# Moving four last-DFT calls of batch 0 out of the transform stage and into the first token tiles

## The chip, the cores and the metric

One core of one Trainium2 chip (runs are compared with runs of the same rounds). The metric is the device time of one execution in microseconds (us). PE is TensorE (matmuls), PEld its weight loads, ACT is ScalarE, DVE is VectorE, POOL is GpSimd, SP is SyncE. "L512" is a line of the kernel. All executions counted here were fast, with a granted TensorE clock of 0.995 to 1.0.

## The reference, cut to what matters

```python
def _attn_ref(x, w_r, w_i, b_r, b_i):            # x: 8 x 3008 x 256
    X = np.fft.rfft(x, axis=1)
    Yr = Xr @ w_r - Xi @ w_i + b_r               # and Yi likewise
    Yr = np.sign(Yr) * np.maximum(np.abs(Yr) - lam, 0.0)
    return np.fft.irfft(Yr + 1j * Yi, n=3008, axis=1)

def _moe_ref(x, w_in, w_out, s, b):              # x: 24064 tokens x 256
    r = np.maximum(x @ w_in, 0.0)                # 256 x 2048
    return (s * (r * r) + b) @ w_out             # 2048 x 256
```

The transforms of length 3008 are done as 94 x 32 by matmuls with DFT tables. "The last DFT" is the final step of the inverse transform; its output `yt` is what the token part reads.

## The kernel before

Batch 0 is transformed first, with only the first units of batch 1 beside it ("the transform stage", up to the first token matmul at 45.56 us). After that come 48 token tiles of 16 slots each. In every slot two matmuls (L781) run, and about four output matmuls (L852) of the tile before. Every second slot ends with one Relu on ACT (L788) and one square (L795 on DVE or L792 on ACT) for both slots. Units of the next batches' transforms are spread over the slots.

The calls that the change moves, cut:

```python
        def last_dft(ec, n):                     # 4 matmuls of 96 columns, 1 evacuation of 128x384
            if ec and n >= HW:                   # HW = 16
                ps = one_bank()                  # pool psf, 2 banks
            elif ec or n >= HW:
                ps = any_bank()                  # psm, psf or psa in turn
            else:
                ps = other_bank() if n % 8 else one_bank()
            for j in range(4):
                ...                              # L512
            evac(yt[:, ec, n : n + 4, :], ..., 384)
...
            for n in {1: (0, 4), 2: (8, 12), 4: (16, 20, 24, 28)}.get(k, ()):
                last_dft(0, n)
...
        rest = [lambda n=n: turn(1, n) for n in range(HW, N2, 4)]
        rest += [lambda n=n: last_dft(1, n) for n in range(HW, N2, 4)]
...
    load.update(act=0.0, dve=0.0)                # at the start of the token tiles
...
    schedule(17, 10, rest[4:])                   # spread over slots 17 to 26
```

Who empties a bank is decided while the program is written, by a running tally of estimated load:

```python
    load = {"act": 0.0, "dve": 0.0}

    def evac(dst, src, cols, scale=None):
        ta, td = 0.17 + cols / 1200.0, 0.15 + cols / 960.0
        if load["act"] + ta <= load["dve"] + td:
            load["act"] += ta
            ...                                  # copy on ScalarE
        load["dve"] += td
        ...                                      # copy on VectorE
...
        # the square of a token tile, same tally
        if load["act"] + 0.25 + w / 600.0 < load["dve"]:
            ...                                  # L792, ScalarE
        else:
            ...                                  # L795, VectorE
```

Of the kernel before, what the change touches and what calls it, by code (L numbers as in the profile page):

```python
# [16 lines left out]
N2 = 32  # L17
# [79 lines left out]
def kernel(  # L97
# [17 lines left out]
    DC = D // P  # L115
# [3 lines left out]
    HW = N2 // 2  # L119
# [45 lines left out]
# [4 lines that stand above are left out]
            if scale is None:  # L169
                return None, nc.scalar.copy(out=dst, in_=src)  # L170
            return None, nc.scalar.mul(out=dst, in_=src, mul=scale)
        load["dve"] += td
        if scale is None:
            return nc.vector.tensor_copy(out=dst, in_=src), None
        return nc.vector.tensor_scalar_mul(out=dst, in0=src, scalar1=scale), None
# [8 lines left out]
    def any_bank():  # L184

        turn_of[0] += 1
        if "h" in pools:
            return (other_bank, one_bank)[turn_of[0] % 2]()
        return (mix_bank, one_bank, mix_bank, other_bank)[turn_of[0] % 4]()
# [4 lines left out]
    def one_bank():  # L194
        return fpool.tile([P, 512], F32, name="psf", tag="psf")

    def other_bank():
        return apool.tile([P, 512], F32, name="psa", tag="psa")
# [128 lines left out]
    def place_f(q):  # L327

        for a in range(2):
            r = slice(64 * a, 64 * a + 64)  # L330
            copy = nc.scalar.copy if a else nc.vector.tensor_copy
            copy(out=blocks(F_t)[r, q, :, a], in_=F_c[r, q])
            nc.vector.tensor_scalar_mul(
                out=blocks(F_2[0])[r, q, 0, a], in0=F_c[r, q, 1], scalar1=-1.0
            )
            nc.vector.tensor_copy(out=blocks(F_2[0])[r, q, 1, a], in_=F_c[r, q, 0])
# [26 lines left out]
    def first_batch():  # L363
# [52 lines left out]
        def mix(ec, u):  # L416

            g = vpool.tile([P, 4, 2, P], F16, name="g0", tag="v")
            gs[(ec, u)] = g
            for half in range(2):  # L420
                ps = mix_bank().rearrange("p (j r e) -> p j r e", j=2, r=2)
                for j in range(2):
                    q = 4 * u + 2 * half + j
                    for dc in range(DC):
                        nc.tensor.matmul(  # L425
                            ps[:, j], ut[:, dc, 4 * q : 4 * q + 4, :],
                            W_t[:, dc, :, ec * P : (ec + 1) * P],
                            start=(dc == 0), stop=(dc == DC - 1),
                        )
                if half:  # L430
                    on_act = nc.scalar.copy(out=g[:, 2:4], in_=ps)
                    load["act"] += 0.58
                else:
                    on_dve = nc.vector.tensor_tensor(
                        out=g[:, 0:2], in0=ps,
                        in1=b_g[:, :, ec * P : (ec + 1) * P].unsqueeze(1).to_broadcast(
                            [P, 2, 2, P]
                        ),
                        op=ALU.add,
                    )  # L440
                    load["dve"] += 0.69
            return on_dve, on_act

        def fwd_dft(ec, u):
            ps = one_bank().rearrange("p (j e) -> p j e", j=4)
            g = gs.pop((ec, u))
            for j in range(4):
                q = 4 * u + j
                if j == 2:
                    nc.tensor.matmul(  # L450
                        ps[:, 2:4], sel_t,
                        b_h[:, ec * P : (ec + 1) * P].unsqueeze(1).to_broadcast([P, 2, P]),
                        start=True, stop=False, skip_group_check=True,
                    )
                for r, f in enumerate((F_t[:, q, :], F_2[q // H][:, q % H, :])):
                    nc.tensor.matmul(  # L456
                        ps[:, j, :], f, g[:, j, r, :], start=(r == 0 and j < 2),
                        stop=(r == 1), skip_group_check=True,
                    )
            pos = mpool.tile([P, 4, P], F32, name="m", tag="m")  # L460
            nc.scalar.activation(out=pos, in_=ps, func=AF.Relu, bias=neg_lam)
            z = gpool.tile([P, 4, P], F16, name="z", tag="gt")
            nc.vector.scalar_tensor_tensor(  # L463
                out=z, in0=ps, scalar=LAM, in1=pos, op0=ALU.add, op1=ALU.min
            )
            load["act"] += 0.69
            load["dve"] += 0.69
            zt[(ec, u)] = z

        def inv_dft(ec, u):  # L470
            ps = other_bank()
            z = zt.pop((ec, u))
            for j in range(4):
                nc.tensor.matmul(
                    ps[:, j * P : (j + 1) * P], z[:, j, :], T_t[:, 4 * u + j, :],
                    start=True, stop=True,
                )
            evac(
                vt[:, ec, :, 16 * u : 16 * u + 16],
                ps.rearrange("p (k n) -> p n k", n=N2), 512,  # L480
            )
# [4 lines left out]
        def turn(ec, n):  # L486

            ps = mix_bank() if ec == 0 else any_bank() if n < HW else one_bank()
            for j in range(4):
                nc.tensor.matmul(  # L490
                    ps[0:96, j * P : j * P + P], vt[:, ec, n + j, :], eye_t,
                    start=True, stop=True,
                )
            h, k = divmod(n, HW)
            evac(
                vs[(0, h)][:, k : k + 4, ec * P : (ec + 1) * P],
                ps[0:96].rearrange("p (j e) -> p j e", e=P), 512,
            )
# [2 lines left out]

        def last_dft(ec, n):

            if ec and n >= HW:
                ps = one_bank()
            elif ec or n >= HW:
                ps = any_bank()
            else:
                ps = other_bank() if n % 8 else one_bank()
            for j in range(4):  # L510
                h, k = divmod(n + j, HW)
                nc.tensor.matmul(  # L512
                    ps[:, j * 96 : j * 96 + 96],
                    vs[(0, h)][:, k, ec * P : (ec + 1) * P], C_t,
                    start=True, stop=True,
                )
            evac(
                yt[:, ec, n : n + 4, :],
                ps[:, 0:384].rearrange("p (j n) -> p j n", n=96), 384,
            )  # L520
# [3 lines left out]
        def some(n):  # L524
            for _ in range(n):
                if more:
                    more.pop(0)()

        steps = [(ec, u) for ec in range(DC) for u in range(U)]
        for i in range(2 * U + 2):  # L530
            if i < 2 * U:
                left = mix(*steps[i])
            if i == 0:
                with tc.issue_after(left[0].ins), tc.issue_after(left[1].ins):
                    place_f(slice(4, H))
            if 0 <= i - 1 < 2 * U:
                fwd_dft(*steps[i - 1])
            if 0 <= i - 2 < 2 * U:
                inv_dft(*steps[i - 2])
            k = i - U - 2  # L540
            if 0 <= k < 4:
                turn(0, 8 * k)
                turn(0, 8 * k + 4)
            for n in {1: (0, 4), 2: (8, 12), 4: (16, 20, 24, 28)}.get(k, ()):
                last_dft(0, n)
            if i >= 2 * U:
                some(3)
            if i == 9:

                gate = nc.gpsimd.tensor_copy(out=low[0:1, 0, 0:1], in_=vt[0:1, 1, 0, 0:1])  # L550
                with tc.issue_after(gate.ins):
                    make_w_g()
                    make_bounds()
                    sum_w_out()
# [4 lines left out]
        turn(1, 12)  # L559
        some(1)  # L560
        last_dft(1, 0)
        last_dft(1, 4)
        some(2)
        last_dft(1, 8)
        last_dft(1, 12)

        rest = [lambda n=n: turn(1, n) for n in range(HW, N2, 4)]
        rest += [lambda n=n: last_dft(1, n) for n in range(HW, N2, 4)]
        return rest, more


# [303 lines left out]
    def schedule(start, span, units):  # L875
        for i, u in enumerate(units):
            plan.setdefault(start + (i * span) // len(units), []).append(u)

    with tc.tile_pool(name="psm", bufs=4, space=bass.MemoryType.PSUM) as pool:
        pools["m"] = pool  # L880
        rest, more = first_batch()
# [10 lines left out]
            mark[tl[1]] = i * MC  # L892
    schedule(0, 10, more)
    schedule(10, 6, rest[:4])
    schedule(17, 10, rest[4:])
    plan.setdefault(14, []).append(make_bias)
    plan.setdefault(18, []).append(load_x_2)
    schedule(24, 42, s23_units(1))
# [53 lines left out]
```

## Time and profile before

| | |
|---|---|
| time, median | 846.8 us (846.37 to 847.73, 6 runs) |
| PE, DVE, ACT busy shares | 99%, 82%, 76% |
| first token matmul (L781) | 45.56 us |
| evacuations of the four moved calls | two on DVE, two on ACT, 38.25 to 40.07 us |
| squares on DVE, on ACT | 319, 65 |

The groups of the page that show how the token work is split (line, engine, operation, output<-input, count; then busy us, mean ns of one; then idle time before them and what ended it):

```profile
L788 ACT ACTIVATE rt<-psh 128x1024 f32<-128x1024 f32 (+2 forms) x384 | 387.2, 1009 | 120.2 <-PE psh L781 118.8
L795 DVE TENSOR_TENSOR gt<-rt 128x1024 f16<-128x1024 f32 (+2 forms) x319 | 382.3, 1202 | 94.4 <-ACT rt L788 93.4
L792 ACT ACTIVATE gt<-rt 128x1024 f16<-128x1024 f32 (+2 forms) x65 | 68.2, 1050 | 0.9
```

Both engines spend much of the token stage waiting for PE: PE is the bound there. The rest of the profile is read in the prediction.

### The profile page before, as it was taken

The numbers are of one execution on the slowest core, as the hardware profiler recorded it, in microseconds if no ns is written. First come the engines' busy times: TensorE is split into PE (matmuls) and PEld (weight loads), VectorE is DVE, ScalarE is ACT, GpSimd is POOL, SyncE is SP. The second block draws the span as 40 slices with busy tenths as digits, with TensorE's granted clock in tenths as the row PEclk, the third lists the DMA queues.
The fourth block names the chain that finished last, engine by engine and source line by source line (L and its number), as shares of the span: only waits on it lengthen the run. The fifth ranks groups of instructions, "written<-read, shape, count | busy, mean of one in ns | idle before, by whom it ended". The sixth has DMA issues, their size and how long they took to land.

```text
span 844.6 us, 17119 instructions
## 1 busy us (share of the span) xinstructions
PE 835.1 (99%) x6654; PEld 601.3 (71%) x6654; DVE 694.7 (82%) x1034; ACT 640.6 (76%) x862; POOL 45.9 (5%) x73
## 2 busy tenths in 40 slices
PE   8999999999999999999999999999999999999998
PEld 7857767777677766777677776777667777766765
DVE  5999987888888988888888888798978888776674
ACT  5987887778778877788777787778877778666673
POOL 4630000000000001000000000000000000000000
PEclk9999999999999999999999999999999999999999
DMA  7955467224851367324761247613354223411111
GB/s 200 181 151 118 119 161 199 74 77 98 202 156 54 103 171 188 93 70 107 189 174 50 81 101 196 172 43 90 106 152 125 59 78 97 113 33 38 38 44 50
DMA packets 105939, 96.06 MB, mean 114 GB/s; under 512 B 9607, under 2 KB 97675, under 8 KB 104515
## 3 DMA queue, kind: packets, MB, share of 16 engines
q1 hardware_dynamic: 99362, 80.55, 32.9%
q0 software_dynamic: 6496, 14.42, 10.6%
q8 instruction: 52, 0.85, 0.4%
q14 instruction: 29, 0.23, 0.1%
HBM read 53.52 MB, written 46.66 MB: 119 GB/s over the span
## 4 chain that ended last, share of the span: by engine, by line
PE 92%; ACT 3%; DVE 2%; DMA 1%; issue 1%; POOL 0%; DVEq 0%; ACTq 0%; POOLq 0%
PE psa L852 38%; PE psh L781 37%; PE psf L647 4%; PE psf L582 3%; PE psf L633 2%; PE psf L677 2%; PE psf L618 2%; PE psf L730 2%; ACT rt L788 1%; DMA x<-in_x_dram 1%; PE psm L425 1%; POOL x L213 0%; ACT yt L170 0%; DVE z L463 0%; PE psf L456 0%
## 5 line engine op out<-in xcount | busy, mean ns | idle before, releaser
L788 ACT ACTIVATE rt<-psh 128x1024 f32<-128x1024 f32 (+2 forms) x384 | 387.2, 1009 | 120.2 <-PE psh L781 118.8
L795 DVE TENSOR_TENSOR gt<-rt 128x1024 f16<-128x1024 f32 (+2 forms) x319 | 382.3, 1202 | 94.4 <-ACT rt L788 93.4
L852 PE MATMUL psa<-w_out_t,gt 128*128 128x256 f16 (+1 forms) x3024 | 454.4, 272 | 0.1
L852 PEld LDWEIGHTS <-gt 128*128 128x128 f16 (+1 forms) x3024 | 300.9, 101 | 186.6 <-issue 1.1
L781 PE MATMUL psh<-yt,w_in 128*128 128x512 f16 (+1 forms) x1344 | 396.8, 378 | 0.2 <-ACT rt L788 0.2
L781 PEld LDWEIGHTS <-w_in 128*128 128x128 f16 x1536 | 142.7, 98 | 26.2 <-issue 1.2
L862 DVE SCALAR_TENSOR_TENSOR ost<-psa,s_bc,bias_bc 128x512 f32<-128x512 f32 (+2 forms) x97 | 71.1, 733 | 9.6 <-PE psa L852 7.9
L792 ACT ACTIVATE gt<-rt 128x1024 f16<-128x1024 f32 (+2 forms) x65 | 68.2, 1050 | 0.9
L652 DVE TENSOR_TENSOR ring<-psf,s 128x512 f16<-128x512 f32 x84 | 57.6, 685 | 3.3 <-PE psf L647 3.2
L170 ACT CAST v<-psf 128x512 f16<-128x512 f32 x77 | 44.8, 582 | 19.4 <-PE psf L677 19.4
L170 ACT CAST xf<-psf 128x512 f16<-128x512 f32 x79 | 46.3, 586 | 8.8 <-PE psf L618 8.8
L781 PE MATMUL psh<-tail,w_in 128*128 128x512 f16 (+1 forms) x192 | 52.1, 353 | 0.0
L170 ACT CAST u<-psf 96x512 f16<-96x512 f32 x74 | 42.8, 580 | 11.2 <-PE psf L582 10.9
L647 PE MATMUL psf<-W_g,xf 128*128 128x256 f16 x336 | 50.4, 273 | 0.0
L170 ACT CAST yt<-psf 128x480 f16<-128x480 f32 (+2 forms) x76 | 39.0, 520 | 14.7 <-PE psf L730 14.2
L213 POOL DMA_DIRECT2D x<-in_x_dram x36 | 18.8, 527 | 432.9 <-PE psf L582 431.7
L582 PE MATMUL psf<-x,A_t 94*96 94x512 f16 x102 | 38.9, 382 | 1.0 <-ACT yt L170 0.6
L658 DVE TENSOR_TENSOR ring<-ring,high 128x512 f16<-128x512 f16 x84 | 35.6, 423 | 2.3
L659 DVE TENSOR_TENSOR ring<-ring 128x512 f16<-128x512 f16 x84 | 35.6, 423 | 2.1
L657 DVE TENSOR_TENSOR ring<-ring,low 128x512 f16<-128x512 f16 x84 | 35.5, 422 | 1.6
L647 PEld LDWEIGHTS <-xf 128*128 128x128 f16 x336 | 32.9, 98 | 4.1 <-issue 0.2
L730 PE MATMUL psf<-C_t,vs 96*128 96x96 f16 x448 | 33.2, 205 | 0.0
(100 smaller groups left out, 508.6 us busy)
## 6 DMA issues: line engine op xcount, KB each, us to landing
out_dram<-ost SPq DMA_DIRECT2D x152, 128.0 KB
ud<-u SPq DMA_DIRECT2D x28, 384.0 KB
us<-ud SPq DMA_DIRECT2D x28, 384.0 KB
vd<-v SPq DMA_DIRECT2D x42, 256.0 KB
vs<-vd SPq DMA_DIRECT2D x14, 768.0 KB
x<-in_x_dram POOLq DMA_DIRECT2D x28, 376.0 KB, 6.3
ring<-ring SPq DMA_DIRECT2D x280, 32.0 KB
out_dram<-ost SPq DMA_DIRECT2D x16, 120.0 KB
```

Of the source, the lines that this page charges most:

```text
L170: return None, nc.scalar.copy(out=dst, in_=src)
L582: nc.tensor.matmul(ps[0:96, :], A_t[0:N1, :], x16[(b, c)][0:N1, j * D : (j + 2) * D], start=True, stop=True,)
L647: nc.tensor.matmul(ps[:, r, :], xt[:, 2 - r, dc], W_g[:, dc, r], start=(dc == 0), stop=(dc == DC - 1),)
L652: nc.vector.tensor_tensor(out=t, in0=ps, in1=hold[i // 2][:, i % 2].unsqueeze(1).to_broadcast([P, 2, D]), op=ALU.add,)
L658: nc.vector.tensor_tensor(out=m, in0=m, in1=high, op=ALU.min)
L730: nc.tensor.matmul(ps[:, j * 96 : (j + 1) * 96], vs[(b, h)][:, k, ec * P : (ec + 1) * P], C_t, start=True, stop=True,)
L781: nc.tensor.matmul(o, w_in_t[dc][:, mc * P : (mc + 1) * P], r, start=(dc == 0), stop=(dc == DC - 1),)
L788: nc.scalar.activation(out=rt[:, :, 0:w], in_=ps[:, :, 0:w], func=AF.Relu)
L792: nc.scalar.activation(out=gt[:, :, 0:w], in_=rt[:, :, 0:w], func=AF.Square)
L795: nc.vector.tensor_tensor(out=gt[:, :, 0:w], in0=rt[:, :, 0:w], in1=rt[:, :, 0:w], op=ALU.mult)
L852: nc.tensor.matmul(ps[0:size, h, :], gts[(ti, mc // 2)][:, mc % 2, sub * size : (sub + 1) * size], w_out_t[:, mc, :], start=(mc == 0), sto ...
L862: nc.vector.scalar_tensor_tensor(out=ost[0:size, 0:k], in0=ps[0:size, 0:k], scalar=s_bc[0:size], in1=bias_bc[0:size].unsqueeze(1).to_broad ...
```

## The change

The intent: the transform stage is limited by evacuations, and four of its last-DFT calls are not needed until the fourth token tile (slot 48). So they join the four calls that already lie in the slots. They use the two psf banks there, and the list is spread over 16 slots instead of 10.

```diff
-            if ec and n >= HW:
+            if n >= HW:
                 ps = one_bank()
-            elif ec or n >= HW:
+            elif ec:
                 ps = any_bank()
...
-            for n in {1: (0, 4), 2: (8, 12), 4: (16, 20, 24, 28)}.get(k, ()):
+            for n in {1: (0, 4), 2: (8, 12)}.get(k, ()):
                 last_dft(0, n)
...
-        rest += [lambda n=n: last_dft(1, n) for n in range(HW, N2, 4)]
+        rest += [lambda n=n, e=e: last_dft(e, n) for n in range(HW, N2, 4) for e in range(DC)]
...
-    schedule(17, 10, rest[4:])
+    schedule(17, 16, rest[4:])
```

## The prediction

> **What bounds the kernel now.** I read the page's first part, then busy time by stretch, then the chain that ended last, then the engines' timelines from 30 to 76 us. Columns of the windows view: stretch, length, then busy time and instruction count of PE, PEld, DVE, ACT and POOL, granted clock, DMA share, GB/s.
>
> ```profile
> PE 835.1 (99%) x6654; PEld 601.3 (71%) x6654; DVE 694.7 (82%) x1034; ACT 640.6 (76%) x862; POOL 45.9 (5%) x73
> 30.00:40.00 10.00, 9.79 (x138) 8.63 (x137) 9.78 (x18) 9.83 (x21) 7.68 (x9) 1.00 1.22 195
> 60.00:70.00 10.00, 9.89 (x87) 7.11 (x86) 8.76 (x14) 6.93 (x11) 2.96 (x8) 1.00 0.81 150
> ```
>
> The two stretches have different limits although PE reads 98 to 99% in both. From 30 to 40 us (batch 0's transforms, where the four moved calls end) DVE and ACT are both full, 9.78 and 9.83 of 10 us. From 60 to 70 us (slots about 21 to 34 of the token tiles) ACT has 3.1 us free and DVE 1.2. To see whether PE is really full I replaced its busy time by what its instructions occupy back to back: in an unbroken run, four matmuls of 96 columns take 0.17 us from start to start, one of 256 takes 0.109, one of 512 takes 0.216. Against the starts in the timeline this leaves about 2.2 us of PE holes from 31.5 to 46 us, 1.6 us from 46 to 76, and only 3.3 us in all of 76 to 845. So the time is the PE work plus some holes early on, and a change to the order of early work can act only through those holes.
>
> The chain of waits (start, length, what) shows the first stretch led by evacuations and the later one by PE:
>
> ```profile
> 38.54 0.60 DVE z L463
> 39.14 0.93 DVE yt L174 x2
> 40.07 0.60 DVE u L174
> 40.67 0.61 DVE vt L174
> ...
> 44.85 0.38 PE psf L582
> 45.23 0.22 PE psa L582
> 45.45 0.27 PE psf L582
> 45.72 0.88 PE psh L781 x4
> ...
> 61.91 0.86 ACT rt L788
> 62.77 0.07 issue
> 62.84 0.48 ACT yt L170
> ```
>
> Here "DVE yt x2" is two of the four evacuations that the change moves: 0.93 us on the chain itself. The first token matmul is at about 45.6 us. At 62 us the chain passes through another evacuation of the same kind, the last of the four that already lie in the slots: a PE stop of about 0.3 us there waits for a bank. The moved work on its engines, and the bank it holds:
>
> ```profile
> 39.06 0.54 DVE L174 CAST yt<-psf 128x384 f16<-128x384 f32 x1
> 39.53 0.54 DVE L174 CAST yt<-psa 128x384 f16<-128x384 f32 x1
> ```
>
> ```profile
> 38.25 0.47 ACT L170 CAST yt<-psm 128x384 f16<-128x384 f32 x1
> ...
> 39.09 0.50 ACT L170 CAST yt<-psm 128x384 f16<-128x384 f32 x1
> ```
>
> ```profile
> 38.41 0.33 PE L512 MATMUL psa<-C_t,vs 96*128 96x96 f16 x4
> ...
> 40.12 0.38 PE L474 MATMUL psa<-T_t,z 128*128 128x128 f16 x4
> ```
>
> The psa bank written at 38.41 is emptied by the cast at 39.53, which gives way at 39.99; only then, at 40.12, do the inverse-transform matmuls of the last unit get a bank, though their input z is ready at 39.14. So the moved call delays batch 0's chain twice over: as DVE time and as bank.
>
> **What the Trainium skill says.** "TensorE: Matmul & The Clock Gate", section "Wait — 56ns, not 53.3ns?": start to start is N ÷ 2.4 GHz plus about 2.5 ns warm. That is 42.5, 109 and 216 ns for 96, 256 and 512 columns; the trace agrees (0.17 us per four of 96), and the clock is 1.00 throughout. "Perfetto Trace Analysis", section "Identifying the Most-Contended Engine": matmul busy share is a poor measure, since pipelined instructions overlap. The trace agrees: 9.79 of 10 us busy from 30 to 40, with a hole of 0.38 us after the matmuls at 37.46. The same page, "Matmuls": independent groups should rotate through banks so that one's evacuation overlaps the next one's matmuls. In the slots the moved calls have the two psf banks alone, where before they could use three pools; the stop at 62.8 us is what too few banks look like. "ScalarE: Activation LUTs", section "What ACT_TABLE_LOAD costs": 186 ns plus 0.833 ns per column, overlapping by about 93 ns. For 384 columns that is 506 ns less 93, so 0.41 us effective; the trace has 0.47 to 0.50 us long and 0.36 to 0.37 us from start to start, a little cheaper, and I use the trace.
>
> **The change part by part.** Nothing is deleted: 16 matmuls of 96 columns and four evacuations of 128x384 leave the transform stage and reappear among the token tiles.
>
> Removed from the transform stage. On PE: 4 x 0.17 = 0.68 us, mostly beside the evacuations. On DVE: start 39.06 to start 39.99, 0.93 us. On ACT: 38.25 to 38.61 and 39.09 to 39.46, 0.36 + 0.37 = 0.73 us. Both engines are nearly continuously busy until about 46.3 us (ACT has holes of 0.49 and 0.42 us, DVE none after 32.5), and the evacuation split rebalances by the kernel's own load count. I take the mean of the two, 0.83 us, by which the token tiles start earlier. The bounds are 0.73, and 0.93 if the DVE-led chain alone counts. The rotation over pools is not disturbed: four fewer calls are one whole turn of a cycle of four.
>
> Added in the slots. The list spread from slot 17 grows from four calls over 10 slots to eight over 16: slots 17, 19, 21 and so on to 31. On PE: 16 x 0.0425 = 0.68 us, in a stage where PE has few holes, so I count it as fully on the path. On ACT or DVE: about 4 x 0.37 = 1.5 us, or 4 x 0.47 = 1.9, beside 3.1 us of ACT and 1.2 us of DVE idle time in this stretch: no bound there. First use of this half is the fourth tile, slot 48, so no deadline is near. The next batch's second-stage input also arrives earlier with the earlier start, since what produces it moves along, so its loads make no new wait.
>
> Sum: -0.83 + 0.68 = -0.15 us. Two smaller terms have opposite signs. The new matmuls can fill part of the holes from 57 to 71 us (0.13, 0.27, 0.12 and 0.28 us, some of which wait for data rather than banks): estimate -0.3 us. The two psf banks are shared with batch 1's units from slot 24: 44 units over 42 slots, about one per slot, and slots 25, 27, 29 and 31 now carry one more. Two or three waits of the size seen at 62.8 us, shortened because some coincide with holes that exist already, are +0.2 us as an estimate. Total -0.25 us; 846.8 becomes about **846.5 us**.
>
> **The rivals.**
> First: the evacuation stage was the whole limit and the slots have room, so the 0.83 us is gained without paying. For it: DVE and ACT full at 30 to 40 us, ACT with 3.1 us free later. Against it: the PE holes in 46 to 76 us add to 1.6 us and several wait on data. The time would be 845.8 to 846.1.
> Second: a bank wait takes the place of the evacuation wait. Every extra psf use in slots 25 to 31 waits behind a Relu of 1.0 us or a square of 1.2 us, and the chain of batch 1's mix (sum, mix, clamp) slips too. For it: the stop at 62.8 us, 0.48 us of yt on the chain. Against it: a stop with one unit per slot is seen only once, and ACT is not full. At 0.3 to 0.4 us for each of four calls, +1.2 to +1.6 on top of -0.15 makes 847.9 to 848.3.
> Third: the evacuation choice is a running count of ACT and DVE load; four more entries can flip later choices for the whole kernel (65 squares on ACT, 319 on DVE now). After 76 us PE has 3.3 us of holes in all, so a reshuffle can gain or lose some tenths, rarely 1 us. It would move the time by -0.6 to +0.8 without any cause in the change itself.
> Fourth: the start of the token tiles does not move, because ACT's remaining queue or a psm bank sets it. Then the 0.68 us of PE work is a plain loss: 847.3 to 847.5. The chain through 39.14 to 40.67 speaks against it.
>
> **Range and chances.** The sum is -0.25. The first rival reaches down to -1.0, the fourth and part of the second and third up to +0.8. Eight times in ten I expect 845.7 to 847.4. A change of 2% is 16.9 us; all the work moved is 0.68 us of PE and 1.66 us of evacuation, and all holes up to 76 us are a few us, so neither 2% side is within reach: faster 0.01, same 0.98, slower 0.01.
>
> **What would show each step right or wrong.** Right: the first token matmul starts 0.7 to 0.9 us earlier than 45.56; the two yt casts are gone from DVE before 40 us and the inverse-transform matmuls of the last unit start near 39.3 rather than 40.12; the lead shrinks to 0 to 0.4 us by the end of the second tile, about 76 us, and stays there. PE holes from 31.5 to 46 us are smaller by little, since work and time both leave. Wrong: if the first token matmul moves by under 0.4 us, the transform stage had another limit (fourth rival). If the lead is still 0.7 us at 76 us, the slots had room (first rival). If new PE holes before psf matmuls appear at slots 25 to 31, ended by yt, xf or ring evacuations, it is the second rival. If the lead changes by more than 0.4 us after 80 us, it is the third, and the tally of squares on ACT would differ from 65.

## The result, and the profile after

The changed kernel took 847.46 us (847.16 to 848.62, 6 runs) against 846.8. The ratio is 1.0009, 95% interval 0.9996 to 1.0021: "same" at the 2% limit, but 0.06 us above the range that I gave. (Ratios here are the mean time of one kernel's fast runs over that of the other's in the same rounds, so not quite the ratio of the medians.)

The time by stretch after, in the columns explained in the prediction:

```profile
30.00:40.00 10.00, 9.86 (x130) 8.24 (x127) 9.79 (x17) 9.82 (x21) 6.74 (x8) 1.00 1.21 194
...
60.00:70.00 10.00, 9.92 (x92) 6.99 (x90) 8.25 (x14) 7.25 (x11) 2.92 (x8) 1.00 0.73 136
```

ACT and DVE are as full as before from 30 to 40 us; from 60 to 70 us ACT has taken 0.32 us more and DVE is 0.5 us less busy. Neither of the two is near a limit there. The first token matmuls, on PE, before and after:

```profile
45.34 0.38 PE L582 MATMUL psf<-x,A_t 94*96 94x512 f16 x1
45.56 1.89 PE L781 MATMUL psh<-yt,w_in 128*128 128x512 f16 x8
```

```profile
39.59 0.39 PE L474 MATMUL psa<-T_t,z 128*128 128x128 f16 x4
...
44.52 0.59 PE L781 MATMUL psh<-yt,w_in 128*128 128x512 f16 x2 [0.30 <-ACT yt L170]
44.95 0.38 PE L582 MATMUL psa<-x,A_t 94*96 94x512 f16 x1
45.17 0.38 PE L582 MATMUL psf<-x,A_t 94*96 94x512 f16 x1
```

The last unit's inverse transform gets its bank at 39.59 instead of 40.12 (the forecast said near 39.3), and the token tiles start at 44.52 instead of 45.56. That is 1.04 us earlier, more than the 0.7 to 0.9 forecast. Part of it is order: three of batch 1's L582 matmuls, which stood before the first token matmul, now stand behind it (two are shown). The lead does not last, for ACT then has a copy for batch 1 to finish before the first Relu. ACT before, then after:

```profile
46.76 1.94 ACT L788 ACTIVATE rt<-psh 128x1024 f32<-128x1024 f32 x2 [0.42 <-PE psh L781]
```

```profile
45.58 0.58 ACT L170 CAST u<-psf 96x512 f16<-96x512 f32 x1 [0.63 <-PE psf L582]
46.31 1.94 ACT L788 ACTIVATE rt<-psh 128x1024 f32<-128x1024 f32 x2
```

The first Relu is at 46.31 instead of 46.76, so only 0.45 us of that lead gets through to it (0.62 from equal starts, explained below). And the split of the squares has changed, as the groups of the page after show:

```profile
L788 ACT ACTIVATE rt<-psh 128x1024 f32<-128x1024 f32 (+2 forms) x384 | 387.1, 1009 | 114.6 <-PE psh L781 112.9
L795 DVE TENSOR_TENSOR gt<-rt 128x1024 f16<-128x1024 f32 (+2 forms) x323 | 386.5, 1200 | 102.5 <-ACT rt L788 101.5
...
L792 ACT ACTIVATE gt<-rt 128x1024 f16<-128x1024 f32 (+2 forms) x61 | 64.2, 1053 | 1.1
```

Four squares more are on DVE, four fewer on ACT, though nothing in the diff touches squares.

**Where the time went.** I took the start of every L781 and L852 matmul from both traces and subtracted that of the same-numbered matmul of the kernel before. One correction is needed: the first matmul of the forward transform (L456) starts at 16.44 us before and at 16.61 after, and in the 14 traces it starts anywhere from 16.24 to 17.81 us, in kernels that are alike up to there. So I count every lag from that matmul. Negative is ahead of the kernel before; the columns are times in the kernel before.

| lag, us | 50 us | 76 us | 115 us | 347 us | 569 us | 840 us |
|---|---|---|---|---|---|---|
| changed kernel | -0.62 | -0.10 | -0.70 | +0.01 | +0.64 | +0.94 |

The moved work is over by 73 us, and there the change is 0.10 us ahead. It even gains 0.6 more by 115 us. Then it loses 1.64 us between 200 and 740 us, in steps of 0.1 to 0.5 us, at work that the diff does not mention.

I then evaluated the tally of both kernels. Of 822 choices between ACT and DVE, 117 come out differently: 4 in the transform stage, 26 in token tiles 0 to 5 (up to about 145 us; two of these are the moved calls' own) and 87 later. The build also sets each engine's order of instructions. PE's order differs between the two kernels only up to 72 us and in one matmul at 107 us; from 109 us on it is identical.

**Theory R:** the four extra entries in the tally flip later choices; a flipped choice delays an evacuation, and PE waits for its bank. **Rival B:** the moved calls cost bank waits in their own slots. **Rival N:** the lag is chance of single runs.

### The profile page after: what moved, and what is told of

It is laid out like the page before. It is cut to its first block, busy times and chain, and to the rows that moved or that the text cites. A ratio compares the mean times of both kernels' runs of the same rounds, so it can differ in the third digit from the quotient of the medians.

```text
span 845.7 us, 17135 instructions
## 1 busy us (share of the span) xinstructions
PE 835.7 (99%) x6654; PEld 601.7 (71%) x6654; DVE 693.3 (82%) x1031; ACT 641.9 (76%) x865; POOL 45.4 (5%) x73
## 4 chain that ended last, share of the span: by engine, by line
PE 90%; DVE 3%; ACT 3%; issue 1%; DMA 1%; POOL 0%; DVEq 0%; SPq 0%; ACTq 0%; POOLq 0%
PE psa L852 36%; PE psh L781 36%; PE psf L647 4%; PE psf L582 2%; PE psf L618 2%; PE psf L633 2%; PE psf L677 2%; PE psf L730 2%; ACT rt L788 1%; DVE gt L795 1%; PE psm L425 1%; DMA x<-in_x_dram 1%; PE psf L456 1%; ACT yt L170 0%; DVE ring L652 0%
## 5 line engine op out<-in xcount | busy, mean ns | idle before, releaser
L795 DVE TENSOR_TENSOR gt<-rt 128x1024 f16<-128x1024 f32 (+2 forms) x323 | 386.5, 1200 | 102.5 <-ACT rt L788 101.5
L852 PE MATMUL psa<-w_out_t,gt 128*128 128x256 f16 (+1 forms) x3024 | 454.3, 273 | 0.1
L852 PEld LDWEIGHTS <-gt 128*128 128x128 f16 (+1 forms) x3024 | 300.9, 101 | 186.7 <-issue 1.4
L781 PE MATMUL psh<-yt,w_in 128*128 128x512 f16 (+1 forms) x1344 | 396.8, 378 | 0.4 <-ACT yt L170 0.3
L781 PEld LDWEIGHTS <-w_in 128*128 128x128 f16 x1536 | 142.5, 98 | 27.2 <-issue 2.3
L792 ACT ACTIVATE gt<-rt 128x1024 f16<-128x1024 f32 (+2 forms) x61 | 64.2, 1053 | 1.1
L652 DVE TENSOR_TENSOR ring<-psf,s 128x512 f16<-128x512 f32 x84 | 57.5, 684 | 3.8 <-PE psf L647 3.5
L170 ACT CAST u<-psf 96x512 f16<-96x512 f32 x84 | 48.7, 580 | 14.1 <-PE psf L582 13.9
L781 PE MATMUL psh<-tail,w_in 128*128 128x512 f16 (+1 forms) x192 | 52.1, 353 | 0.0
L582 PE MATMUL psf<-x,A_t 94*96 94x512 f16 x102 | 38.9, 381 | 1.4 <-ACT yt L170 0.5
```

The costliest lines, as they stand in the source:

```text
L170: return None, nc.scalar.copy(out=dst, in_=src)
L582: nc.tensor.matmul(ps[0:96, :], A_t[0:N1, :], x16[(b, c)][0:N1, j * D : (j + 2) * D], start=True, stop=True,)
L652: nc.vector.tensor_tensor(out=t, in0=ps, in1=hold[i // 2][:, i % 2].unsqueeze(1).to_broadcast([P, 2, D]), op=ALU.add,)
L781: nc.tensor.matmul(o, w_in_t[dc][:, mc * P : (mc + 1) * P], r, start=(dc == 0), stop=(dc == DC - 1),)
L792: nc.scalar.activation(out=gt[:, :, 0:w], in_=rt[:, :, 0:w], func=AF.Square)
L795: nc.vector.tensor_tensor(out=gt[:, :, 0:w], in0=rt[:, :, 0:w], in1=rt[:, :, 0:w], op=ALU.mult)
```

## The experiments

In the "choices" experiments the tally is replaced by a fixed list, one letter per choice in program order, put together call by call from the two kernels:

```diff
-    load = {"act": 0.0, "dve": 0.0}
+    load, picks = {"act": 0.0, "dve": 0.0}, iter("ADADADADADADADADAADAADADAADAD...")
...
-        if load["act"] + ta <= load["dve"] + td:
+        if next(picks) == "A":
...
-        if load["act"] + 0.25 + w / 600.0 < load["dve"]:
+        if next(picks) == "A":
```

All lags found, counted as above (the last column is the median time, with that of the kernel before in the same rounds):

| run | 50 us | 76 us | 115 us | 347 us | 569 us | 840 us | time / before |
|---|---|---|---|---|---|---|---|
| after_again | -0.63 | -0.10 | -0.71 | +0.02 | +0.65 | +0.95 | 847.74 / 846.78 |
| before_new_choices | 0.00 | +0.13 | -0.46 | +0.26 | +0.90 | +1.20 | 847.67 / 846.78 |
| removal_only | -0.63 | -0.62 | -0.63 | -0.62 | -0.63 | -0.63 | 846.13 / 846.78 |
| addition_only | 0.00 | +0.52 | -0.08 | -0.09 | -0.09 | -0.10 | 846.90 / 846.64 |
| mixed_choices | -0.63 | -0.11 | -0.71 | -0.71 | -0.72 | -0.73 | 846.09 / 846.64 |
| after_old_choices | -0.62 | +1.14 | +1.14 | +1.14 | +1.14 | +1.14 | 847.07 / 846.78 |
| after_old_choices_2 | -0.63 | +0.23 | +0.23 | +0.23 | +0.22 | +0.21 | 847.19 / 846.64 |
| late_w_sum | 0.00 | +1.52 | +1.52 | +1.52 | +1.51 | +1.50 | 846.82 / 846.64 |
| two_squares_swapped | -0.01 | -0.02 | -0.01 | -0.01 | +0.43 | +0.42 | 847.32 / 846.55 |
| head_start_05 | 0.00 | -0.54 | -1.05 | -0.40 | -0.13 | +0.16 | 848.21 / 846.55 |
| head_start_10 | +0.56 | +0.47 | +0.47 | +0.74 | +0.88 | +0.88 | 847.86 / 846.55 |
| head_start_20 | -0.28 | -0.02 | +0.04 | +0.70 | +0.69 | +0.69 | 847.43 / 846.55 |

A word on noise: every timed comparison here has a 95% interval of about 0.12 to 0.18% either side, 1.0 to 1.5 us. All are "same" at the 2% limit, and only that of head_start_05 (1.0003 to 1.0033) leaves out no change at all. So what carries the argument are the lags, which repeat to 0.02 us where the program repeats, save for one accident described below. The kernel before has a single trace, but four runs that end with its choices (removal_only, addition_only, mixed_choices, late_w_sum) stay parallel to it to 0.02 us from 347 us to the end.

**The changed kernel again** (no edit).

> The changed kernel once more, for the spread and to see whether the curve of its lag behind the kernel before repeats. Theory R (the changed tally of ScalarE and VectorE load reshuffles later choices of engine, and PE waits a little more for psf banks after 200 us): again 847.2 to 847.9, about 0.7 over before, and in the trace a lead of 0.4 to 0.7 us at 120 us that turns into a lag of 0.9 to 1.3 us by 735 us, in steps at the same places (304 to 307, 322 to 328, 512, 533, 564, 729 us). Theory N (the lag is chance of one run): the steps fall elsewhere or are absent, and the mean is within 0.3 of before.

847.74 us, ratio 1.0008 (0.9995 to 1.0021). The lags are those of the first trace to 0.02 us in every column. Rival N falls.

**The kernel before with the changed kernel's choices in the token tiles.** Edit: the list above, and nothing moved.

> The kernel before, all four calls left in the transform stage, but in the token tiles every choice of engine is the one that the changed kernel made. Theory R: slower than before by 0.7 to 1.2 us, 847.5 to 848.0, with the steps after 200 us where the changed kernel has them. Rival B: as before, 846.6 to 847.0, since nothing was moved.

847.67 us, ratio 1.0008 (0.9994 to 1.0022). Nothing was moved, and the end lags by 1.20 us, with the losses where the changed kernel has them: from 115 us to the end it loses 1.66 us, the changed kernel 1.64. PE's order differs from the kernel before only in four matmuls, at 64 to 66 and 107 us, so the loss after 115 us is one of engine choices alone. This is theory R by itself.

**The changed kernel with the old choices in the token tiles.** Edit: the list; the four moved evacuations stay on ACT.

> The changed kernel, but in the token tiles every choice between ScalarE and VectorE is the one that the kernel before made for the same call; the four moved evacuations stay on ScalarE. Instruction orders are then those of before from the third tile on. Theory R: the steps after 120 us vanish, the time is 846.1 to 846.8 (0 to 0.7 under before, my predicted -0.25 in the middle). Rival B (the moved calls themselves cost bank waits in slots 17 to 31): the lag is there by 80 us and the time stays at 847.3 to 848. Theory N: no difference from the changed kernel.

847.07 us, ratio 1.0002 (0.9989 to 1.0014). Half of this was a miss. The later steps are gone, as R says: the lag is flat from 76 us on. But it is flat at +1.14, which Rival B would claim. The trace shows what happened. POOL's last addition of the output weights and DVE's squares, in that order:

```profile
47.30 1.16 POOL L344 TENSOR_TENSOR w_sum<-acc,w_out_t 128x512 f16<-128x512 f32 x1
```

```profile
47.38 5.57 DVE L795 TENSOR_TENSOR gt<-rt 128x1024 f16<-128x1024 f32 x4 [1.26 <-ACT rt L788]
```

Four squares took 5.57 us instead of 4.67: the first alone took 2.17. It issued 0.08 us after POOL's addition, which ends at 48.46, and finishes 1.09 us after that. In the trace of the kernel before POOL was done at 46.07, well before the first square at 47.8. So I ran the kernel again.

> The same kernel as after_old_choices. Its profiled run was the slowest of five (847.8 against a median of 847.1), and its first square on VectorE took 2.17 us where all others take 1.2, while GpSimd was still adding rows of the output weights, late because those weights had landed late. If that was an accident of the one run: the first square takes 1.2 us here, and the lag at 76 us falls from 1.14 to 0.2 to 0.5 us (from equal starts), flat afterwards. If the old choices cause it: again a lag of 1.1 at 76 us.

An accident of that one execution. Here POOL was done at 46.95 and the four squares took the usual time:

```profile
47.77 4.67 DVE L795 TENSOR_TENSOR gt<-rt 128x1024 f16<-128x1024 f32 x4 [1.26 <-ACT rt L788]
```

The lag at 76 us is +0.23, and flat after it. 847.19 us, ratio 1.0006 (0.9988 to 1.0024). So the old choices cost 0.33 us in the slots that now carry the moved calls (+0.23 against -0.10), and they also keep the old holes between 82 and 105 us. My expected 846.1 to 846.8 was wrong for that reason. What makes the 0.33 is not separated: beside the choices, PE's order came out differently, with 24 matmuls moved within 62 to 67 us. That the tally adapts to the moved calls is a guess.

**POOL's sums made late on purpose.** Edit, in the kernel before:

```diff
-        for q in range(2, MC, 2):
+        for q in [2, 2, 2] + list(range(4, MC, 2)):
```

> The kernel before with GpSimd's first addition done three times instead of once, so that its chain of sums ends about 2.5 us later, at about 48.5 us instead of 46.1, over VectorE's first squares (from 47.8 us). If GpSimd's additions and VectorE's two-input squares hold each other up: one or two squares of about 2 us instead of 1.2, and a time 0.3 to 0.9 over before. If not: squares of 1.2 us and no change in time.

Median 846.82 us, ratio 0.9999 (0.9983 to 1.0014). In the trace the collision is there, twice, and each engine stops the other. DVE, then POOL:

```profile
47.63 5.06 DVE L795 TENSOR_TENSOR gt<-rt 128x1024 f16<-128x1024 f32 x3 [1.32 <-ACT rt L788]
```

```profile
43.52 4.86 POOL L344 TENSOR_TENSOR acc<-acc,w_out_t 128x512 f32<-128x512 f32 x4
48.45 2.02 POOL L344 TENSOR_TENSOR w_sum<-acc,w_out_t 128x512 f16<-128x512 f32 x1
```

The first three squares took 1.83, 2.18 and 1.21 us, and POOL's last addition 2.02 instead of 1.16. The lag is 1.5 us. The Trainium skill says this in "SBUF — State Buffer", section "SBUF: two separate sides": an exclusive lock between a DVE instruction with two SBUF inputs and a GpSimd instruction that reads SBUF; whoever starts second blocks for the whole instruction. The trace agrees, with these lengths; an overlap of 0.16 us by the profile, in after_again, lengthened nothing (1.23 us). Yet by the times only the profiled execution paid: 847.84 us, against 846.57, 846.77 and 846.87 for the other three. Why the others did not is open, since they have no trace. For the question at hand it means that this collision can spoil a profile; in the two traces of the changed kernel it did not happen (first squares of 1.23 us).

**The removal alone.** Edit, in the kernel before, with the old choices in the token tiles; a wrong result (relative error 0.11):

```diff
-            for n in {1: (0, 4), 2: (8, 12), 4: (16, 20, 24, 28)}.get(k, ()):
+            for n in {1: (0, 4), 2: (8, 12)}.get(k, ()):
...
+    plan.setdefault(22, []).append(
+        lambda: nc.gpsimd.memset(yts[0][:, 0, HW:], 0.0)
+    )
```

> Wrong result on purpose: the four calls are taken out of the transform stage and not put anywhere (their part of the output buffer is zeroed by GpSimd, which is idle then); all choices in the token tiles as in the kernel before. It measures the first term of the sum. The prediction: first token matmul 0.7 to 0.9 us earlier, time lower by 0.8, 845.9 to 846.2. If another limit holds the transform stage (the fourth rival): under 0.3 us gained, 846.5 or more.

846.13 us, ratio 0.999 (0.9978 to 1.0003). The first token matmul is 1.22 us early, more than the 0.7 to 0.9 predicted, for it stands ahead of three L582 matmuls here too. The fifth, with two of the three ahead of it again, is 0.79 us early; by the 17th, where the order is equal again, the lead is 0.63 us and stays there for the whole kernel. That is the lead of the first Relu, which stands behind the copy shown above.

**The addition alone.** Edit, in the kernel before: the four calls stay, and are done again in the slots.

```diff
-        rest += [lambda n=n: last_dft(1, n) for n in range(HW, N2, 4)]
+        rest += [lambda n=n, e=e: last_dft(e, n, True) for n in range(HW, N2, 4) for e in range(DC)]
...
-    schedule(17, 10, rest[4:])
+    schedule(17, 16, rest[4:])
```

(with `again=True` they take a psf bank, as in the changed kernel; the choices are the changed kernel's up to tile 5, then the old ones).

> The kernel before with the four calls left where they are and done a second time in the slots (a right result, the same values written again), with the changed kernel's choices up to the sixth tile and those of before from there. It measures the second term: my prediction counted 0.68 us of TensorE work plus a net of -0.1 for holes filled and bank waits. Expected from the traces so far: lag of 0.5 to 0.6 us at 76 us (removal gave -0.62 and both together -0.10), then 0.6 less by 115 us from the choices; time 846.6 to 847.0. If bank waits take the place (the second rival): lag of 1.2 or more at 76 us and a time above 847.6.

846.90 us, ratio 1.0005 (0.9988 to 1.0022). 16 matmuls of 0.0425 us are 0.68 us of PE work, and the lag at 76 us is 0.52: the slots absorb 0.16. The sum with the removal is -0.62 + 0.52 = -0.10, exactly the changed kernel's lag at 76 us, and at 115 us -0.63 - 0.08 = -0.71. The two parts add up, with nothing left over. Rival B falls: with the tally's own choices the moved calls cost less than their matmuls. The PE holes agree: those over 60 ns between 52 and 76 us that a yt or xf evacuation ended add to 0.54 us before and 0.55 us after the change. (The 0.52 includes the flipped choices of the first tiles, which alone make +0.13 at 76 us, in before_new_choices.)

**The changed kernel's order, its own choices up to tile 5, the old ones after.** Edit: the list.

> The changed kernel with its own choices of engine up to the sixth token tile (about 125 us), and from there on the choices of the kernel before. The order of TensorE's instructions is exactly that of the changed kernel. Theory R (the lag comes from later choices): the lead of 0.7 us at 115 us (counted from equal starts of the transform stage) stays flat to the end; time 846.0 to 846.4, faster than both kernels, by 0.4 to 0.7 than before. If the lag has another cause after 125 us: 847.2 or more, like the changed kernel.

846.09 us, ratio 0.9992 (0.9976 to 1.0008). PE's instruction order is identical to the changed kernel's; only ACT and DVE differ, and only from tile 6 on, which starts at 145 us (not 125, as I wrote). The lag stays at -0.71 to -0.73 to the end. Matmul by matmul against the changed kernel, the difference of 1.67 us is made of ten steps of added lag, of 0.05 to 0.53 us (2.35 together), and four back (0.67). Every one stands at a matmul into psf, and what released each of the ten in the changed kernel is, by the profile, an evacuation of psf: ring, v or yt. So the wait for a bank that theory R names is there at every step. This is the version that beats both kernels in the traces, by 0.7 us over the kernel before and 1.7 over the changed one; the timed gain of 0.55 in the medians is not clear of noise.

**Two squares exchanged in the kernel before.** To see one step with nothing else around it: the fifth square of tile 29 goes to ACT and the eighth to DVE, as in the changed kernel; the 820 other choices are the old ones.

> The kernel before with two of its 384 squares exchanged between the engines, as the changed kernel has them: in token tile 29 the fifth square goes from VectorE to ScalarE and the eighth from ScalarE to VectorE. TensorE's order is the same. Theory R in its narrow form (a square put on VectorE delays the evacuation that frees a psf bank, and TensorE waits for it): the trace is level with before, counted from equal starts, until 562 us, then one step of 0.3 to 0.4 us at 564 us, and level after it; time 0.3 to 0.4 over before. If a step needs the whole changed history and not just its neighbours: no step, same time.

A step of 0.35 us at 563 us, and level after it. (A step of 0.09 at 543 us stands before the exchanged squares, the first of which is at 552 us, so it is not theirs; the 0.43 in the table holds both.) 847.32 us, ratio 1.0008 (0.9993 to 1.0023). PE's order is the same in both. The trace of the kernel before at that place, DVE and then PE (start in that trace's own time, length, engine, line, and in brackets the idle time just before and what ended it):

```profile
560.26 0.68 DVE L652 TENSOR_TENSOR ring<-psf,s 128x512 f16<-128x512 f32 x1
560.87 1.22 DVE L795 TENSOR_TENSOR gt<-rt 128x1024 f16<-128x1024 f32 x1
...
562.77 0.39 PE L618 MATMUL psf<-F_t,us 128*128 128x128 f16 x4
```

With the two squares exchanged:

```profile
561.21 1.22 DVE L795 TENSOR_TENSOR gt<-rt 128x1024 f16<-128x1024 f32 x1
562.35 0.68 DVE L652 TENSOR_TENSOR ring<-psf,s 128x512 f16<-128x512 f32 x1
...
563.08 0.38 PE L618 MATMUL psf<-F_t,us 128*128 128x128 f16 x4 [0.19 <-DVE ring L652]
```

And the changed kernel:

```profile
561.73 1.22 DVE L795 TENSOR_TENSOR gt<-rt 128x1024 f16<-128x1024 f32 x1
...
562.86 0.68 DVE L652 TENSOR_TENSOR ring<-psf,s 128x512 f16<-128x512 f32 x1
...
563.60 0.38 PE L618 MATMUL psf<-F_t,us 128*128 128x128 f16 x4 [0.19 <-DVE ring L652]
```

L652 reads the mix result out of a psf bank. Where it comes ahead of the square, the bank is free 1.8 us before PE asks for it; where a second square has been put on DVE just before, L652 is last in line and PE stops for it. Another step, at 729 us, is of the same family with a copy instead of a square. Before, then after:

```profile
729.12 0.55 ACT L170 CAST yt<-psf 128x480 f16<-128x480 f32 x1
729.12 0.66 DVE L174 CAST yt<-psf 128x480 f16<-128x480 f32 x1 [1.09 <-PE psf L730]
```

```profile
729.22 1.01 ACT L170 CAST yt<-psf 128x480 f16<-128x480 f32 x2
...
729.82 0.37 PE L730 MATMUL psf<-C_t,vs 96*128 96x96 f16 x5 [0.20 <-ACT yt L170]
```

Two banks filled together are emptied by two engines at once, or by one after the other.

**The tally disturbed and nothing else.** Three kernels with the one edit below, for 0.5, 1.0 and 2.0:

```diff
-    load.update(act=0.0, dve=0.0)
+    load.update(act=0.5, dve=0.0)
```

> The kernel before with nothing moved and nothing added: only the tally of ScalarE load starts the token tiles at 0.5 instead of 0. 105 of the later choices of engine come out differently. Theory R: the bookkeeping alone moves the end by some tenths either way, between -0.7 and +1.5 us, in steps of 0.1 to 0.5, each at a wait for a psf bank. If choices of engine hardly matter and the changed kernel's lag needs its own order of work: within 0.1 us of before in the trace.

> As head_start_05, with a start of 1.0 for ScalarE; 48 choices differ, fewer than in the changed kernel (117). Theory R: again steps, fewer of them, an end between -0.5 and +1.0 us of before in the trace.

> As head_start_05, with a start of 2.0 for ScalarE; 31 choices differ, all or nearly all early. Theory R: the trace runs level with before once the choices agree again, an end between -0.6 and +0.6 us.

105, 48 and 31 choices differ, and with them the place of 11, 3 and 40 matmuls in PE's order, so these runs show what the tally does by every way it has, not by engine choice alone. The +0.56 and -0.28 at 50 us arise at 45 us, at the first flipped copies. The ends lag by 0.16, 0.88 and 0.69 us. Ratios: 1.0018 (1.0003 to 1.0033), 1.0015 (1.0000 to 1.0029), 1.0008 (0.9991 to 1.0024). The expectation for 2.0 was a miss by 0.1 us in size, and its differing choices were not nearly all early: 27 of the 31 lie among the first 354 of the 822, and the lag is indeed level from 347 us on; the four later ones cost nothing. That 0.5 first leads by 1.05 us and then gives it all back is the changed kernel's pattern without the change. Its four times (847.02, 847.39, 849.04, 849.45) spread more than its trace explains; that stays open. None of the three draws, nor the changed kernel's, beats the kernel before at the end. Whether it holds a good draw, four others are too few to say.

## Why the prediction was right or wrong

- The bound: right. Evacuations set the pace up to 46 us and PE after it. The lag moves only where PE waits.
- Removed from the transform stage, "the mean of the two, 0.83 us": 1.22 at the first token matmul and 0.79 at the fifth (both partly by order), 0.62 from the 17th on. The term was too large by 0.21; the first Relu, not the first matmul, carries the lead on.
- Added in the slots, +0.68 for PE, -0.3 for holes filled and +0.2 for bank waits, so +0.58: measured +0.52. Right within 0.06, in part by luck: the two small terms were not measured apart, and the 0.52 holds flipped choices of the first tiles. With the old choices the same addition makes 0.85 (-0.62 to +0.23).
- The sum of the moved work, -0.25: measured -0.10 at the end of the second tile, inside the "0 to 0.4" of lead that I said would show it right; the lead did not stay. Nor is the worth of the move one number. With the changed kernel's choices in both, it gains 0.26 us by the end (+0.94 against +1.20 in before_new_choices), close to my sum; with the old choices in both, it loses 0.21.
- First rival (gain without paying): false, 0.52 of 0.62 us is paid back. Second (bank waits in the slots): false for the changed kernel; with the old choices forced on it the slots cost 0.33 us more, not 1.2 to 1.6, and whether by bank waits is not separated. Fourth (the start does not move): false.
- The step that failed is the third rival: "After 76 us PE has 3.3 us of holes in all, so a reshuffle can gain or lose some tenths, rarely 1 us. It would move the time by -0.6 to +0.8". It came true, and I had left it out of the sum. Its size was 0.60 gained up to 115 us and 1.64 lost after it, +1.04 in all. The holes that exist bound what a reshuffle can gain; they say nothing on what it can lose, since each flipped choice can open a hole that was not there. With -0.10 for the moved work that makes +0.94, which is the lag of the changed kernel. Its own test had been named ("if the lead changes by more than 0.4 us after 80 us ... the tally of squares on ACT would differ from 65"), and it is 61. The tally could also have been worked out from the text of the diff; I counted it as chance instead.
- Two readings were off without effect on the sum: 60 to 70 us are slots 20 to 29, not 21 to 34 (the second tile runs from 54.8 to 73.3 us), and the clock is not 1.00 "throughout": the trace grants 0.50 from 8.9 to 12.3 us, before the stretches that I used.

## What to carry to other kernels

When a kernel decides at build time, by a running tally, which engine does what, any edit that adds or drops an entry re-decides everything behind it; measure an edit with those choices held fixed, at the old list and at the new one, and tune the choices as a change of their own. A small gain where work was moved can be real and still vanish: compare the starts of same-numbered instructions along the whole kernel, from a common start, before blaming the moved work. A stage that hardly waits has more to lose from a reshuffle than to gain: here, after 145 us, 2.35 us of steps in lag stand against 0.67 back.

## What the Trainium skill lacked or had wrong

- "Perfetto Trace Analysis", "Optimizing Scalar/DVE Operations": it says that some work can go to either engine, and not that which one matters through the order of instructions on it. Two squares exchanged, at equal counts, cost 0.35 us of PE time here.
- The same section gives about 51 ns of access overhead for Scalar and 125 ns for DVE on PSUM. Here ACT copies of 384 and 512 columns, back to back, measured 0.358 and 0.465 us from start to start, which is 0.84 ns a column and about 0.04 us fixed (an estimate from the two) and roughly agrees; DVE copies measured 0.465 and 0.598, which is 1.04 ns a column and about 0.07 us fixed, so 125 ns is too much here.
- "SBUF — State Buffer", "SBUF: two separate sides", was right on the lock between POOL and DVE. A size to add: a square of 1.22 us became 2.17 us, and an addition on POOL of 1.16 us became 2.02. That, by the times, it struck the profiled execution and not the others (847.84 against 846.57 to 846.87) is on none of the pages that I used.
- No page that I used gives the scatter of a kernel's start: the same matmul began at 16.24 to 17.81 us in 14 traces, a scatter as large as the effect studied here.
